# Moving attention masks in the DVE queue, and some copies, banks and biases of the first halves, in a fused attention and feed-forward kernel

## The chip, the cores and the metric

The kernel runs on one core of a Trainium2 chip. A core has a matrix engine (TensorE, PE in the profile), a vector engine (VectorE, DVE), a scalar engine (ScalarE, ACT), GpSimd (POOL) and a queue engine for transfers (SyncE, SP). Each works through its own instructions in the order in which they were written, and engines wait for one another by semaphores. Matrix products are written to banks of PSUM; all else lies in SBUF. The metric is the device time of one execution in microseconds; the median of ten runs is given.

## The reference

Attention over 4 batches of 8 heads with 768 positions of 64 numbers. A query sees the first 8 keys and the 96 keys that end at itself, with a slope on the distance; the heads' outputs, side by side, are rows of 512 for a gated feed-forward layer with 1536 inner columns.

```python
scores = scale * np.matmul(q, k.transpose(0, 1, 3, 2))
is_global = pos[None, :] < int(n_global)
is_local = (rel >= 0) & (rel < int(n_local))
keep = is_global | is_local
dist = np.where(is_global & ~is_local, float(n_local), np.abs(rel).astype(np.float32))
bias = -slopes[:, None, None] * dist[None, :, :]
scores = np.where(keep, scores + bias, -1000000000.0)
a = np.exp(scores - np.max(scores, axis=-1, keepdims=True))
a = a / (np.sum(a, axis=-1, keepdims=True) + 1e-09)
attn = np.matmul(a, v)
...
gate = np.maximum(x @ w_gate, 0.0)
val = x @ w_val
return (gate * val @ w_out).astype(np.float32)
```

## The kernel before

The work is cut into eight halves (`s` or `c`, 0 to 7): half a sequence of one batch, 384 queries. Within a half, heads go in four pairs (`p`), and the keys that a half's queries can see lie in tiles of 120 with the 8 global keys in front of each. The scores of one pair lie in three banks (`g`, 0 to 2) with keys on the partitions.

A pair passes these steps. Its q and k are cast to bf16 (`piece_cast`) and transposed: in half 0, 1 and 2 by PE (`piece_t`, L299) and copied out of PSUM (`piece_copy_k`, L278 to L284, `piece_copy_q`, L315), in halves 3 to 7 by transfers that transpose (`early_pieces`). Then come the scores. In half 0, and for pairs 0 and 3 of half 1, the bias is first put into the banks by products of a scaled identity with the distances (`piece_bias`, L327), scores are added on top (`piece_scores`, L342), and ScalarE takes the exponential (`piece_exp`, L359). Everywhere else `piece_qk` computes plain scores (L411) and the exponential (L414), and `piece_mask` (L429) multiplies by a table of exponentials of the bias on VectorE (`m_all`, made for each head by `setup_mask`, L245). Halves 0 and 1 do the product with the values and with ones by `piece_av_wide` (L480), take the sum's Ln and the exponential of its negative on ScalarE (`piece_ln_wide` L497, `piece_inverse_wide` L502), and VectorE multiplies (`piece_mul_wide`, L508) to give `xT`, the feed-forward input. From half 2 on `piece_av` (L445, L454, L459) and `piece_norm` (L465) do the same.

The feed-forward of a half is 12 steps `gate(fc)` and `val(fc)` of four products each (L531); ScalarE applies Relu (`grelu`, L540), VectorE multiplies into `ht` (L547), and then output products go over the 12 columns (L554, in the last block L569). `F0[2*fc]` and `F0[2*fc+1]` are gate and val of half 0; `gate[i]` and `val[i]` are the first four of them.

PSUM has eight banks in three pools: three for scores (`qk_psum`), two for values and transposes (`av_psum`), three for the feed-forward (`ff_psum`). A bank is used again when its last reader is done.

The order of every engine's work is the order of the calls. The first two halves are written out by hand call by call (from L627 on). After that `weave` puts items of attention between feed-forward steps by their share of the work: half 2's transposes (`T2`) with the feed-forward of halves 0 and 1; `attention_pieces(2)` with the end of these; then the attention of half c + 1 with the feed-forward of half c. In `attention_pieces` each item is one bank of scores with its mask, one value product, or one normalisation:

```python
return (QK(0) + QK(1) + AV(0) + N(0) + QK(2) + AV(1) + N(1) + g[0:1] + a[0:1] + g[1:2] + a[1:2]
        + N(2) + g[2:3] + [(0.0, lambda: None)] + AV(3) + N(3))
```

Loads come from two queues. SP loads q and k of half 0 and of halves 3 to 7. POOL issues, in this order: values of batch 0, part of q and k of half 1, the first quarter of the gate weights in two parts, the rest of q and k, the first part of the value weights (`wv0`), more values, the second and third parts of both weights, q and k of half 2, the output weights.

Of the kernel before, what the change touches and what calls it, by code (L numbers as in the profile page):

```python
# [8 lines left out]
FP32 = mybir.dt.float32  # L9
# [6 lines left out]
def kernel(  # L16
# [12 lines left out]
    nc = tc.nc  # L29
# [8 lines left out]
    HP = H // 2  # L38
# [13 lines left out]
    banks_of_half = [[], []]  # L52
# [191 lines left out]
    def setup_mask(h):  # L244
        nc.scalar.activation(m_all[:, h], dd, AF.Exp, bias=0.0, scale=-slopes[h])  # L245
# [42 lines left out]
    def piece_t(s, p, pool=av_psum, name="av_ps", apart=False):  # L288
        for i in (1, 0):
            if i == 1 or apart:  # L290
                tp = pool.tile([128, 512], FP32, name=name)
                tp = tp[:, 0:QH].bitcast(BF16).rearrange("d (i t) -> d i t", i=2)
            tp_of[s, p, i] = tp[:, i, :]
            for n in range(NN):
                for e in range(2 if s == 1 else 1):
                    r = slice(64 * e, 64 * e + 64) if s == 1 else slice(0, 128)
                    src = (qk16[s, i][:, 2 * p + e, n * D : (n + 1) * D] if s == 1
                           else cast_of[s, p][:, i, n])
                    nc.tensor.matmul(tp[r, i, n * 128 : (n + 1) * 128],  # L299
                                     lhsT=src, rhs=ident, is_transpose=True,  # L300
                                     start=((i == 1 or apart) and n == 0),
                                     stop=((i == 0 or apart) and n == NN - 1))

    def piece_copy_k(s, p):
        b, half = divmod(s, 2)
        put_keys(nc.vector.tensor_copy, nc.vector.tensor_copy, kT[b % 2][p], tp_of[s, p, 1], half)

    def piece_copy(s, p):
        piece_copy_k(s, p)
        piece_copy_q(s, p)  # L310

    def piece_copy_q(s, p, copy=nc.vector.tensor_copy):
        for e in range(2):
            r = slice(64 * e, 64 * e + 64)
            copy(qTb[s % 2][r, p, e, :], tp_of[s, p, 0][r, :])  # L315

    qk_of = {}

    def piece_bias(s, p):
        pool, name = (ff_psum, "ff_ps") if s == 0 and p % 2 else (qk_psum, "qk_ps")  # L320
        banks = [pool.tile([128, 512], FP32, name=name) for _ in range(3)]
        qk_of[s, p] = banks
        for g, bank in enumerate(banks_of_half[s % 2]):
            c = 0
            for i, (j, a, w, m) in enumerate(bank):
                for e in range(2):
                    nc.tensor.matmul(banks[g][:, c : c + NN * w], lhsT=sid[:, 2 * p + e],  # L327
                                     rhs=dd[:, 0 if j == 0 else 1, :, m : m + w],
                                     start=(i == 0 and e == 0), stop=False, skip_group_check=True)
                    c += NN * w  # L330
# [30 lines left out]
    def piece_biased(s, p):  # L361
        piece_scores(s, p)
        for g in range(3):
            piece_exp(s, p, g)
# [33 lines left out]
    def piece_qk(s, p, g, later=None):  # L398
        b, half = divmod(s, 2)
        kt = kT[b % 2][p]  # L400
        qd = qTb[s % 2][:, p].rearrange("d e (n p) -> d e n p", n=NN)
        bank = banks_of_half[half][g]
        cols = sum(2 * NN * w for _, _, w, _ in bank)
        ps = qk_psum.tile([128, 512], FP32, name="qk_ps")
        if g == 0:
            es01_of[s, p] = es_pool.tile([128, 2, 480], BF16, name="es01")
        es = es01_of[s, p][:, g] if g < 2 else es_pool.tile([128, 480], BF16, name="es2")
        c = 0
        for j, a, w, m in bank:
            n_ = 2 * NN * w  # L410
            nc.tensor.matmul(ps[:, c : c + n_], lhsT=kt[:, j, :],  # L411
                             rhs=qd[:, :, :, a : a + w], start=True, stop=True)
            c += n_
        nc.scalar.activation(es[:, 0:cols], ps[:, 0:cols], AF.Exp, bias=0.0, scale=scale)  # L414
        if later is None:
            piece_mask(s, p, bank, es)
        else:
            later.append(lambda: piece_mask(s, p, bank, es))
# [15 lines left out]
    def piece_av(s, p, e):  # L434
        b, half = divmod(s, 2)
        h = 2 * p + e
        vb = vbuf[b % 2]
        av = av_psum.tile([128, 512], FP32, name="av_ps")
        av_of[s, p, e] = av
        av3 = av[:, 0:QH].rearrange("d (n p) -> d n p", n=NN)  # L440
        todo = [t for bank in banks_of_half[half] for t in bank]
        for i, (j, a, w, m) in enumerate(todo):
            es, c = es_of[s, p, j, e]
            z0 = 2 * D * h + (D if e == 0 else 0)
            nc.tensor.matmul(av3[:, :, a : a + w],  # L445
                             lhsT=vb[:, j, z0 : z0 + 128],
                             rhs=es[:, c : c + NN * w].rearrange("k (n p) -> k n p", n=NN),
                             start=(i == 0), stop=(i == len(todo) - 1),
                             skip_group_check=True)
        o0, d0 = (0, 64) if e == 0 else (64, 0)  # L450
        if e == 0:
            av_of[s, p, "l"] = rc_pool.tile([128, QH], FP32, name="lnd")
        ln = av_of[s, p, "l"]
        nc.scalar.activation(ln[o0 : o0 + 64], av[d0 : d0 + 64, 0:QH], AF.Ln, bias=0.0, scale=1.0)  # L454
        if e == 1:
            if s not in xT_of:
                xT_of[s] = xt_pool.tile([128, N_DC, QH], BF16, name="xT")
            rc = rc_pool.tile([128, QH], FP32, name="rcp")
            nc.scalar.activation(rc, ln, AF.Exp, bias=0.0, scale=-1.0)  # L459
            av_of[s, p, "r"] = rc  # L460
            piece_norm(s, p, 0)
# [25 lines left out]
    def piece_norm_wide(s, p):  # L487
        piece_sums_wide(s, p)
        piece_mul_wide(s, p)
# [10 lines left out]
    def piece_inverse_wide(s, p):  # L500
        rc = rc_pool.tile([128, QH], FP32, name="rcp")
        nc.scalar.activation(rc, av_of[s, p, "l"], AF.Exp, bias=0.0, scale=-1.0)  # L502
        av_of[s, p, "r"] = rc

    def piece_mul_wide(s, p):
        if s not in xT_of:
            xT_of[s] = xt_pool.tile([128, N_DC, QH], BF16, name="xT")
        nc.vector.tensor_tensor(xT_of[s][:, p, :], av_of[s, p][1][:, 0:QH], av_of[s, p, "r"], op=ALU.mult)  # L508

    def attention_pieces(s):  # L510
        QK = lambda p: [(0.18, lambda g=g: piece_qk(s, p, g)) for g in range(3)]
        AV = lambda p: [(0.29, lambda e=e: piece_av(s, p, e)) for e in range(2)]
        N = lambda p: [(0.0, lambda: piece_norm(s, p, 1))]
        g = QK(3)
        a = AV(2)
        return (QK(0) + QK(1) + AV(0) + N(0) + QK(2) + AV(1) + N(1) + g[0:1] + a[0:1] + g[1:2] + a[1:2]
                + N(2) + g[2:3] + [(0.0, lambda: None)] + AV(3) + N(3))

# [94 lines left out]
    F0 = [f for _, f in f1_0]  # L615
# [5 lines left out]
    QKB, FFB, AVB = (qk_psum, "qk_ps"), (ff_psum, "ff_ps"), (av_psum, "av_ps")  # L621

    def AV(s, p, *pools):
        piece_av_wide(s, p, *pools)
        piece_norm_wide(s, p)
# [28 lines left out]
    piece_t(0, 2)  # L654
    cast(0, 3, A, A)
    piece_biased(0, 1)
    piece_bias(0, 2)
    piece_copy(0, 2)
    piece_t(0, 3)
    piece_biased(0, 2)  # L660
    piece_copy(0, 3)
    piece_bias(0, 3)
# [15 lines left out]
    def TC(s, p, *pool):  # L678
        piece_t(s, p, *pool)
        piece_copy(s, p)  # L680

    gate, val = F0[0:8:2], F0[1:8:2]
# [4 lines left out]
    piece_mul_wide(0, 0)  # L687
    piece_inverse_wide(0, 1)
    piece_inverse_wide(0, 2)
    piece_t(1, 0)  # L690
    piece_av_wide(0, 3, QKB, FFB)
    piece_ln_wide(0, 3)
    piece_copy_k(1, 0)
    piece_mul_wide(0, 1)
    piece_copy_q(1, 0)
    piece_inverse_wide(0, 3)
    piece_bias(1, 0)
    piece_t(1, 1)
    piece_mul_wide(0, 2)
    piece_mul_wide(0, 3)  # L700
    piece_copy(1, 1)
# [14 lines left out]
    masks = {p: [] for p in (1, 2)}  # L716
    for g in range(3):
        piece_qk(1, 1, g, masks[1])
    setup_mask(5)
    piece_copy(1, 2)  # L720
    gate[3]()
    piece_copy(1, 3)
    for g in range(3):
        piece_qk(1, 2, g, masks[2])
    for f in masks[1]:
        f()
    val[0]()
    piece_bias(1, 3)
    piece_biased(1, 3)
    val[1]()  # L730
    piece_av_wide(1, 0)
    piece_ln_wide(1, 0)
    piece_av_wide(1, 1, QKB)
# [13 lines left out]
    piece_inverse_wide(1, 2)  # L747
    piece_ln_wide(1, 3)
    piece_mul_wide(1, 2)
    piece_inverse_wide(1, 3)  # L750
    piece_mul_wide(1, 3)
    F0[9]()
    F0[10]()
    F0[11]()
    for p in range(HP):
# [7 lines left out]
    for p in range(HP):  # L763
        cast(2, p, P, P)
    load_v_half(2)
    T2 = [(0.0, lambda p=p: TC(2, p, *QKB)) for p in range(HP)]
    weave(f1_1[G[0]] + f1_0[G[1]][4:] + f1_1[G[1]],
          [(0.05 + 0.06 * j, lambda j=j: fill_ones(nc.vector, 0, j)) for j in range(NT)],
          [(0.1 + 0.2 * i, lambda h=h: setup_mask(h)) for i, h in enumerate((0, 1, 6, 7))],
# [50 lines left out]
```

## Time and profile before

| what | value |
|---|---|
| median of 10 runs | 247.32 us (247.06 to 248.03) |
| the profiled execution | 248.0 us, span 246.2 us |
| PE | 238.2 us busy, 97% of the span |
| ACT | 157.5 us, 64% |
| DVE | 135.5 us, 55% |
| POOL | 91.6 us, 37% |
| largest groups on PE | L531 gate 77.9 us, L531 val 77.9 us, L554 63.2 us |
| chain that ended last | PE 85%, DVE 4%, DMA 4%, POOL 3%, ACT 2% |

The span runs from the first to the last instruction; the execution's own time is 1.8 us longer. The sum of busy times of one engine counts products that overlap in the pipeline only once, but the mean duration of a product (326 ns for 128x384) holds its way through the array as well; the distance between two starts is what it costs. The granted clock of PE is full in every part of the span. An idle time in brackets in a timeline names the engine and tile that ended it.

### The profile page before, as it was taken

The numbers are of one execution on the slowest core, as the hardware profiler recorded it, in microseconds if no ns is written. First come the engines' busy times: TensorE is split into PE (matmuls) and PEld (weight loads), VectorE is DVE, ScalarE is ACT, GpSimd is POOL, SyncE is SP. The second block draws the span as 40 slices with busy tenths as digits, with TensorE's granted clock in tenths as the row PEclk, the third lists the DMA queues.
The fourth block names the chain that finished last, engine by engine and source line by source line (L and its number), as shares of the span: only waits on it lengthen the run. The fifth ranks groups of instructions, "written<-read, shape, count | busy, mean of one in ns | idle before, by whom it ended". The sixth has DMA issues, their size and how long they took to land.

```text
span 246.2 us, 4850 instructions
## 1 busy us (share of the span) xinstructions
PE 238.2 (97%) x1739; PEld 143.5 (58%) x1739; DVE 135.5 (55%) x355; ACT 157.5 (64%) x329; POOL 91.6 (37%) x213
## 2 busy tenths in 40 slices
PE   7888999999999999999999999999999999999994
PEld 3674666656454666556654666556665666556644
DVE  6877757966531566336762567427663466523410
ACT  7998764377553877567774877567774778553311
POOL 8996944924680076302546063503620000000000
PEclk9999999999999999999999999999999999999999
DMA  6999999997699776838359959838431100020012
GB/s 179 194 166 183 207 289 232 146 103 244 146 168 173 232 120 151 92 91 252 82 114 98 265 153 147 77 104 258 108 85 70 60 0 3 4 110 18 0 43 86
DMA packets 76536, 32.35 MB, mean 131 GB/s; under 512 B 55424, under 2 KB 73216, under 8 KB 76512
## 3 DMA queue, kind: packets, MB, share of 16 engines
q0 software_dynamic: 34896, 10.27, 37.4%
q1 hardware_dynamic: 41616, 21.78, 33.4%
q8 instruction: 13, 0.21, 0.4%
q14 instruction: 11, 0.09, 0.1%
HBM read 28.38 MB, written 6.29 MB: 141 GB/s over the span
## 4 chain that ended last, share of the span: by engine, by line
PE 85%; DVE 4%; DMA 4%; POOL 3%; ACT 2%; issue 1%; POOLq 0%; DVEq 0%
PE ff_ps L531 47%; PE ff_ps L554 24%; PE av_ps L445 6%; PE qk_ps L411 5%; DMA wg<-in_moe_w_gate_dram 4%; DVE ht L547 2%; POOL vbuf L149 1%; ACT es L414 1%; PE ff_ps L569 1%; DVE qT L315 1%; PE av_ps L480 1%; DVE kT L278 1%; PE qk_ps L480 1%; PE av_ps L299 0%; POOL ks L126 0%
## 5 line engine op out<-in xcount | busy, mean ns | idle before, releaser
L531 PE MATMUL ff_ps<-xT,wg 128*128 128x384 bf16 x384 | 77.9, 326 | 0.8 <-DMA wg<-in_moe_w_gate_dram 0.4
L531 PE MATMUL ff_ps<-xT,wv 128*128 128x384 bf16 x384 | 77.9, 326 | 0.0
L540 ACT ACTIVATE grelu<-ff_ps 128x384 bf16<-128x384 f32 x96 | 46.7, 488 | 34.5 <-PE ff_ps L531 16.8
L547 DVE TENSOR_TENSOR ht<-ff_ps,grelu 128x384 bf16<-128x384 f32 x96 | 53.1, 554 | 23.6 <-PE ff_ps L531 22.0
L554 PE MATMUL ff_ps<-wo_sb,ht 128*128 128x512 bf16 x276 | 63.2, 379 | 0.5 <-DVE ht L547 0.5
L429 DVE TENSOR_TENSOR es<-es,m_all 128x432 bf16<-128x432 bf16 (+5 forms) x118 | 33.7, 316 | 34.6 <-ACT es L414 33.2
L531 PEld LDWEIGHTS <-wg 128*128 128x128 bf16 x384 | 35.9, 97 | 23.5 <-issue 1.0
L531 PEld LDWEIGHTS <-wv 128*128 128x128 bf16 x384 | 36.4, 98 | 22.3 <-DMA wv<-in_moe_w_val_dram 0.2
L414 ACT ACTIVATE es<-qk_ps 128x432 bf16<-128x432 f32 (+2 forms) x78 | 41.0, 532 | 8.2 <-PE qk_ps L411 6.0
L465 DVE TENSOR_TENSOR xT<-av_ps,rcp 64x384 bf16<-64x384 f32 x48 | 26.7, 555 | 33.8 <-ACT rcp L459 21.1
L554 PEld LDWEIGHTS <-ht 128*128 128x128 bf16 x276 | 26.0, 97 | 28.6 <-issue 0.6
L454 ACT ACTIVATE lnd<-av_ps 64x384 f32<-64x384 f32 x48 | 23.3, 485 | 13.3 <-PE av_ps L445 12.5
L367 POOL CAST kc<-ks 128x384 bf16<-128x384 f32 x20 | 9.5, 520 | 57.7 <-DMA ks<-in_k_dram 57.7
L559 ACT COPY osb<-ff_ps 128x512 f32<-128x512 f32 x23 | 13.5, 585 | 24.5 <-PE ff_ps L554 24.3
L411 PE MATMUL qk_ps<-qT,kT 128*128 128x432 bf16 (+5 forms) x118 | 26.7, 286 | 0.1
L149 POOL DMA_DIRECT2D vbuf<-in_v_dram x29 | 24.8, 872 | 0.0
L445 PEld LDWEIGHTS <-vbuf 128*128 128x128 bf16 x216 | 17.8, 98 | 6.4
L445 PE MATMUL av_ps<-es,vbuf 128*128 128x216 bf16 (+4 forms) x216 | 20.5, 226 | 0.0
L411 PEld LDWEIGHTS <-kT 128*128 128x128 bf16 x118 | 11.4, 98 | 8.1
L375 POOL CAST qz<-qs 128x192 bf16<-128x192 f32 x40 | 12.8, 369 | 3.7 <-DMA qs<-in_q_dram 3.7
L459 ACT ACTIVATE rcp<-lnd 128x384 f32<-128x384 f32 x24 | 12.5, 522 | 0.8
L278 POOL COPY kT<-kN 128x360 bf16<-128x360 bf16 x8 | 4.4, 547 | 7.7 <-DMA kN<-kc 7.7
(107 smaller groups left out, 154.0 us busy)
## 6 DMA issues: line engine op xcount, KB each, us to landing
out_dram<-osb SPq DMA_DIRECT2D x23, 256.0 KB
ks<-in_k_dram SPq DMA_DIRECT2D x5, 768.0 KB
qs<-in_q_dram SPq DMA_DIRECT2D x5, 768.0 KB
vbuf<-in_v_dram POOLq DMA_DIRECT2D x23, 120.0 KB, 4.9
wv<-in_moe_w_val_dram POOLq DMA_DIRECT2D x3, 512.0 KB, 10.9
wo_sb<-in_moe_w_out_dram POOLq DMA_DIRECT2D x1, 1536.0 KB, 21.5
wg<-in_moe_w_gate_dram POOLq DMA_DIRECT2D x2, 512.0 KB, 10.6
ks<-in_k_dram SPq DMA_DIRECT2D x4, 192.0 KB
```

Source lines behind the costliest of these rows:

```text
L149: nc.gpsimd.dma_start(out=v_dst(b, NG + r0, NG + r0 + n, j), in_=v[b, :, KT * j + r0 : KT * j + r0 + n, :].rearrange("h p d -> p h d"))
L411: nc.tensor.matmul(ps[:, c : c + n_], lhsT=kt[:, j, :], rhs=qd[:, :, :, a : a + w], start=True, stop=True)
L414: nc.scalar.activation(es[:, 0:cols], ps[:, 0:cols], AF.Exp, bias=0.0, scale=scale)
L429: nc.vector.tensor_mul(e4, e4, mk)
L445: nc.tensor.matmul(av3[:, :, a : a + w], lhsT=vb[:, j, z0 : z0 + 128], rhs=es[:, c : c + NN * w].rearrange("k (n p) -> k n p", n=NN), star ...
L454: nc.scalar.activation(ln[o0 : o0 + 64], av[d0 : d0 + 64, 0:QH], AF.Ln, bias=0.0, scale=1.0)
L465: nc.vector.tensor_tensor(xT_of[s][r, p, :], av_of[s, p, e][r, 0:QH], av_of[s, p, "r"][r], op=ALU.mult)
L531: nc.tensor.matmul(st[key][:, 0:QH], lhsT=w_of(w, dc, fc), rhs=xT_of[c][:, dc, :], start=(dc == 0), stop=(dc == N_DC - 1))
L540: nc.scalar.activation(gr, psg[:, 0:QH], AF.Relu, bias=0.0, scale=1.0)
L547: nc.vector.tensor_tensor(ht[:, fc, :], psv[:, 0:QH], st["r", fc], op=ALU.mult)
L554: nc.tensor.matmul(ps2, lhsT=ht[:, fc, n * 128 : (n + 1) * 128], rhs=wo_sb[:, fc, :], start=(fc == 0), stop=(fc == N_FC - 1))
L559: nc.scalar.copy(osb, ps2)
```

## The change

Four things are changed.

- In `attention_pieces` the mask products of a bank are no longer written right after its exponential, but kept in a list, and written after the scores and the exponential of the next bank, or ahead of the next value product (`flush`). The empty item ahead of the last pair's value products becomes a `flush`. This concerns halves 2 to 7.
- The transposes of half 2 use two banks for a pair, one for k and one for q (`apart=True`), and q is copied out by ScalarE instead of VectorE.
- In half 1, pair 0's transposes go to a bank of `qk_psum` instead of `av_psum`; its q copy comes ahead of half 0's xT product of pair 1; pair 1's transposes come ahead of pair 0's bias. In half 0 the third bank of pair 2's bias is written after pair 3's transposes.
- `val[1]` comes ahead of the bias and scores of half 1's pair 3, the mask table of head 5 after the exponentials of pair 2, and `F0[9]` (`val(4)` of half 0) ahead of the last inverse and xT product of half 1; on PE its place stays the same, on DVE its ht product now stands ahead of that xT product.

The instructions of PE are as many as before. ACT has eight copies more and DVE eight fewer. The orders of POOL and SP are the same.

```diff
-    def piece_bias(s, p):
+    def piece_bias(s, p, groups=(0, 1, 2)):
...
-        for g, bank in enumerate(banks_of_half[s % 2]):
+        for g in groups:
+            bank = banks_of_half[s % 2][g]
...
     def attention_pieces(s):
-        QK = lambda p: [(0.18, lambda g=g: piece_qk(s, p, g)) for g in range(3)]
-        AV = lambda p: [(0.29, lambda e=e: piece_av(s, p, e)) for e in range(2)]
+        masks = []
+
+        def qk(p, g):
+            ready = masks[:]
+            masks.clear()
+            piece_qk(s, p, g, masks)
+            for f in ready:
+                f()
+
+        def flush():
+            for f in masks:
+                f()
+            masks.clear()
+
+        QK = lambda p: [(0.18, lambda g=g: qk(p, g)) for g in range(3)]
+        AV = lambda p: [(0.29, lambda e=e: (flush(), piece_av(s, p, e))) for e in range(2)]
...
-                + N(2) + g[2:3] + [(0.0, lambda: None)] + AV(3) + N(3))
+                + N(2) + g[2:3] + [(0.0, flush)] + AV(3) + N(3))
...
-    piece_bias(0, 2)
+    piece_bias(0, 2, (0, 1))
     piece_copy(0, 2)
     piece_t(0, 3)
+    piece_bias(0, 2, (2,))
...
-    piece_t(1, 0)
+    piece_t(1, 0, *QKB)
     piece_av_wide(0, 3, QKB, FFB)
     piece_ln_wide(0, 3)
-    piece_copy_k(1, 0)
+    piece_copy(1, 0)
     piece_mul_wide(0, 1)
-    piece_copy_q(1, 0)
     piece_inverse_wide(0, 3)
+    piece_t(1, 1)
     piece_bias(1, 0)
-    piece_t(1, 1)
...
-    setup_mask(5)
     piece_copy(1, 2)
     gate[3]()
     piece_copy(1, 3)
     for g in range(3):
         piece_qk(1, 2, g, masks[2])
+    setup_mask(5)
     for f in masks[1]:
         f()
     val[0]()
+    val[1]()
     piece_bias(1, 3)
     piece_biased(1, 3)
-    val[1]()
...
     piece_mul_wide(1, 2)
+    F0[9]()
     piece_inverse_wide(1, 3)
     piece_mul_wide(1, 3)
-    F0[9]()
...
-    T2 = [(0.0, lambda p=p: TC(2, p, *QKB)) for p in range(HP)]
+
+    def T2_piece(p):
+        piece_t(2, p, *QKB, apart=True)
+        piece_copy_k(2, p)
+        piece_copy_q(2, p, nc.scalar.copy)
+
+    T2 = [(0.0, lambda p=p: T2_piece(p)) for p in range(HP)]
```

More of the change, by code (lines that the diff above doesn't have):

```diff
@@ L317 @@
     qk_of = {}
-    def piece_bias(s, p):
+    def piece_bias(s, p, groups=(0, 1, 2)):
         pool, name = (ff_psum, "ff_ps") if s == 0 and p % 2 else (qk_psum, "qk_ps")
-        banks = [pool.tile([128, 512], FP32, name=name) for _ in range(3)]
-        qk_of[s, p] = banks
-        for g, bank in enumerate(banks_of_half[s % 2]):
+        if (s, p) not in qk_of:
+            qk_of[s, p] = [pool.tile([128, 512], FP32, name=name) for _ in range(3)]
+        banks = qk_of[s, p]
+        for g in groups:
+            bank = banks_of_half[s % 2][g]
             c = 0
```

## The prediction

> **What bounds the kernel now.** I read the page's busy table first, then the windows, then the timelines of TensorE (PE), VectorE (DVE) and ScalarE (ACT) around every place where PE pauses. One line of the page and three windows:
>
> ```profile
> PE 238.2 (97%) x1739; PEld 143.5 (58%) x1739; DVE 135.5 (55%) x355; ACT 157.5 (64%) x329; POOL 91.6 (37%) x213
> ```
>
> ```profile
> 41.95:50.44 8.49, 8.27 (x66) 5.34 (x65) 8.05 (x28) 3.12 (x8) 8.49 (x13) 1.00 1.48 153
> 50.44:62.06 11.62, 11.16 (x75) 6.94 (x75) 7.31 (x19) 8.89 (x19) 3.55 (x10) 1.00 1.00 180
> ...
> 108.10:240.30 132.20, 132.20 (x865) 78.22 (x864) 68.87 (x164) 83.43 (x170) 29.41 (x80) 1.00 0.43 98
> ```
>
> The columns of a window are its length, then busy time and count of PE, weight loads, DVE, ACT and POOL, the granted clock, DMA share and GB/s. PE sets the time. Since a busy PE need not be at its peak, I go by the distance from one start to the next: four 128x384 products take 0.65 us wherever nothing is waited for (163 ns each), and that holds from 62.06 us to 240.3, where PE waits for nobody. So no reordering can win anything there; it can only win in the first 62 us. There I add up what PE loses, beginning here:
>
> ```profile
> 23.58 0.81 PE L531 MATMUL ff_ps<-xT,wv 128*128 128x384 bf16 x4
> 24.69 1.23 PE L327 MATMUL qk_ps<-dd,sid 128*128 128x72 bf16 x10 [0.30 <-ACT es L414]
> 25.76 0.75 PE L342 MATMUL qk_ps<-qT,kT 128*128 128x144 bf16 x5
> 26.35 0.81 PE L531 MATMUL ff_ps<-xT,wv 128*128 128x384 bf16 x4
> 27.09 0.50 PE L480 MATMUL av_ps<-es,ones 128*64 128x72 bf16 x10
> ...
> 33.20 0.81 PE L531 MATMUL ff_ps<-xT,wv 128*128 128x384 bf16 x4
> 34.15 0.81 PE L531 MATMUL ff_ps<-xT,wg 128*128 128x384 bf16 x4
> ...
> 49.87 0.35 PE L411 MATMUL qk_ps<-qT,kT 128*128 128x432 bf16 x1
> 50.44 0.81 PE L531 MATMUL ff_ps<-xT,wg 128*128 128x384 bf16 x4 [0.22 <-DVE ht L547]
> ```
>
> The reader is to see starts that come later than the one before plus its length. The last bias (24.69) waits for exponentials that free its banks and takes 1.07 us instead of about 0.65; 34.15 comes 0.30 after 33.20 + 0.65; 50.44 comes 0.39 after 49.87 + 0.18. A further 0.10 is lost at 48.58. The last loss is at 62.06, where the first output product should follow at 61.45: 0.61 us, for a bank that DVE frees:
>
> ```profile
> 60.28 0.56 DVE L465 TENSOR_TENSOR xT<-av_ps,rcp 64x384 bf16<-64x384 f32 x1
> 60.87 0.55 DVE L429 TENSOR_TENSOR es<-es,m_all 128x432 bf16<-128x432 bf16 x1
> 61.45 0.56 DVE L547 TENSOR_TENSOR ht<-ff_ps,grelu 128x384 bf16<-128x384 f32 x1
> ```
>
> A mask (L429) stands ahead of the ht product (L547) that frees the bank.
>
> **Last bias and val[1].** Products are only swapped, so PE's own work is unchanged. val[0] starts at 23.58 as before, since its weights land then (issued 12.55, landing 10.9 later). val[1] follows to 24.88. Meanwhile ACT does the exponentials of pair 2 without the mask table of head 5 ahead of them; in the trace that table (23.22) takes 0.45 of queue, and the three exponentials ended at 25.5, so they end at about 25.05, and the last bank is needed near 25.3: no wait. Ten bias products cost 0.65 (eight took 0.55 at 7.10), the scores 0.59, so the next block starts at 24.88 + 0.65 + 0.59 + the 0.09 that it had = 26.2 instead of 27.09: gain 0.89. It needs values that land at 26.0 (issued 18.8, 7.2 to landing) only 0.4 after its start. The moved table is ready near 25.5; its reader, the masks of pair 2 on DVE, comes after 26.
>
> **F0[9] ahead of the last normalisation.** F0[9] started at 31.89; with the gain it would start at 31.0, but its weights land at 31.1 (issued 20.50, 10.6) and a product started 0.13 after such a landing at 23.58: 31.23, gain left 0.66. The three products end at 33.18. Before, the next one waited 0.30 for F0[9]'s ht, which stood behind the last xT product (33.07 to 33.63). Now ht runs in the time in which xT waits for its reciprocal, and xT is needed only by the fourth product. So 0.30 is won: gain 0.96, next start 33.19.
>
> **The third half's transposes.** The first stood at 41.95, now at 40.99. What is late next is a load: q of this half lands at 40.77 and POOL's cast of its first pair runs from 40.78 to 41.29. Three k transposes run to 41.16, the q ones start at 41.35, and the block ends at 41.52 instead of 42.28: gain 0.76. The load's issue was itself held 0.42 by an exponential that now ends earlier; that could give up to 0.4 back, which I leave out of the sum. Then eight q copies leave DVE, 0.35 each, 2.8 of the 8.05 us it was busy in the 8.49 us window; DVE had 1.9 us of work in each 1.63 us round, now 1.2. The 0.10 and 0.39 go: gain 0.49. On ACT each copy costs 0.464 (the two of the first half). A round there is a relu and a pair of copies, 0.45 + 0.95 = 1.4 of 1.63, and once a mask table of 0.5, 0.3 over; that relu comes late, but its bank is asked for only a product later, over 0.3 away. Between 0 and 0.3 I take 0, as the cover is larger. Two banks for each transpose instead of one: the second's q needs the first's k copied, 0.6 us of DVE work in 1.3 us.
>
> **Queued masks, half 2.** In DVE's new order the ht at 61.45 stands right behind the xT at 60.28, hence 60.87 to 61.43, and PE goes on at 61.48 instead of 62.06 less shift: 0.57 of the 0.61.
>
> **Queued masks, halves 3 to 7.** A gain is excluded by the window to 240.3. A loss would be a value product that finds its mask late. The closest is the last pair's third mask: now one slot (about 1 us) ahead of its reader instead of two. But in both orders it stands right after the same two xT products on DVE, so it starts no later. Ends: 0 and one whole mask (0.5) for each of six halves, 3.0; I take 0.
>
> **First and second half, before 19.5 us.** The transposes of pair 0 need no longer wait 0.63 for a Ln, the bias of pair 0 waits instead for the q copy (16.4), the split bias lets three transposes wait up to 0.2 for ACT's cast. All of it lies ahead of the gate weights, which land at 19.46 (issued 10.36, 9.1). PE reaches them about 18.4 by these rows, so 1.0 us of cover; without it each would count in full. POOL's and SP's orders, and so all loads, are unchanged.
>
> **The sum.** 0.76 + 0.49 + 0.57 = 1.82 us. Against the profiled execution: 248.0 - 1.8 = 246.2, its span 246.2 - 1.8 = 244.4, 1.8 lying around it. That execution is 0.7 above the median of ten, so the median becomes 247.32 - 1.82 = 245.5.
>
> **A rule weighed.** The rows above say that late loads take 10 to 15 us: q of the third half, issued 25.77, lands 15.0 later, and this swallows 0.20 of the gain. The Trainium skill, "DMA: Bandwidth & Descriptors", section Anatomy of one DMA, fits a transfer by 2.0 us plus bytes over 436 GB/s: for 768 KB an estimate of 3.8 us. By it neither load would hold anything, F0[9] would start at 31.0 and the sum would be 0.89 + 0.30 + 0.49 + 0.57 = 2.25 us, 245.1. The fit is for one transfer; here many share the engines, so the rows decide.
>
> **Rivals.** *Loads decide* (0.13): everything up to 42 us is held by the transfers, which share one another's time, and arriving earlier wins nothing. For it: PE sits on landings at 19.46 and 23.45 already. Against: the q row allows 0.76. Then 0.49 + 0.57: 246.3. *ScalarE becomes the gate* (0.08): the copies delay relus, the 0.49 is not won and 0.3 comes on top: 247.32 - 0.76 - 0.57 + 0.3 = 246.3. Against it: 3.12 busy of 8.49. *Waits are replaced* (0.08): at each place another operand is late, under 0.5 won: 247.0. For it: several margins are 0.1 to 0.4 us. *Late masks, slower* (0.09): in halves 2 to 7 the value products of the last pair wait for the third mask. It outweighs 1.82 from 0.30 a half on; at 0.4 it is 6 x 0.4 - 1.82 = +0.6: 247.9. For it: ACT is 63% busy there and the mask waits for its exponential; against it: the same DVE neighbours.
>
> **How the numbers follow.** The forecast has 0.62, with its own range 244.9 (no load holds) to 246.1. What this kernel's measurement can tell from no change is about 0.2%, 0.5 us. Faster: 0.62 + 0.13 + 0.08 = 0.83; same 0.08; slower 0.09. The range takes in the first three cases with 0.3 for unknown ends: 244.8 to 246.6; about 0.17 lies outside.
>
> **What would show it.** Right: the normaliser products of the second half start near 26.2; the first product of its second stage near 33.2; no wait between the third half's transposes and its scores; the output product follows without a DVE wait; after 62 us everything is the same, shifted. Wrong: PE waits after 62 us for L429's masks, or a transpose at 41 us that waits longer than 0.2 for POOL.

## The result and the profile after

The changed kernel takes 246.0 us (median of 16 runs, 245.47 to 246.45). The kernel before, run beside it, takes 247.38 us (58 runs). The ratio is 0.9939, with a 95% interval from 0.9931 to 0.9948. The gain is 1.38 us by medians, where 1.82 was forecast. The profiled execution took 245.88 us, span 244.1, so it stands for the median well; the profiled execution of before, 248.0, did not.

The page's busy line and the windows that answer to those of before (length, then busy time and count of PE, weight loads, DVE, ACT, POOL, the granted clock, DMA share, GB/s), and under them the window of before that answers to the third:

```profile
PE 237.1 (97%) x1739; PEld 143.1 (59%) x1739; DVE 132.7 (54%) x347; ACT 161.0 (66%) x337; POOL 91.2 (37%) x213
```

```profile
39.81:48.56 8.75, 8.24 (x66) 5.37 (x65) 5.88 (x19) 6.62 (x15) 8.47 (x14) 1.00 1.42 176
48.56:59.57 11.01, 11.01 (x77) 6.87 (x76) 6.86 (x18) 8.68 (x18) 3.17 (x6) 1.00 1.24 192
59.57:77.61 18.04, 17.87 (x103) 9.01 (x101) 6.32 (x15) 9.17 (x18) 10.11 (x26) 1.00 1.01 167
106.00:238.15 132.15, 132.15 (x864) 78.15 (x863) 68.11 (x164) 83.42 (x170) 29.17 (x80) 1.00 0.43 98
```

```profile
62.06:79.75 17.69, 17.68 (x100) 8.98 (x100) 5.80 (x14) 8.75 (x18) 8.64 (x21) 1.00 1.03 163
```

Eight q copies have gone from DVE (8.05 us busy before, now 5.88, in the first window) to ACT (3.12, now 6.62). The second window is as long as PE needs: 11.01 of 11.01. The third is new to the story: it was 17.69 long before and is 18.04 now.

The timeline of PE, where the reader should again look for starts that come later than the start before plus its products:

```profile
22.54 1.46 PE L547 MATMUL ff_ps<-xT,wv 128*128 128x384 bf16 x8
23.83 0.77 PE L329 MATMUL qk_ps<-dd,sid 128*128 128x72 bf16 x10
24.45 0.76 PE L344 MATMUL qk_ps<-qT,kT 128*128 128x144 bf16 x5
25.13 0.50 PE L482 MATMUL av_ps<-es,ones 128*64 128x72 bf16 x10
...
31.36 0.81 PE L547 MATMUL ff_ps<-xT,wv 128*128 128x384 bf16 x4
32.01 0.81 PE L547 MATMUL ff_ps<-xT,wg 128*128 128x384 bf16 x4
...
39.81 0.33 PE L299 MATMUL qk_ps<-ident,qk 128*128 128x128 bf16 x3
40.65 0.34 PE L299 MATMUL qk_ps<-ident,qk 128*128 128x128 bf16 x3 [0.51 <-POOL qk L263]
...
48.38 0.35 PE L413 MATMUL qk_ps<-qT,kT 128*128 128x432 bf16 x1
48.56 0.81 PE L547 MATMUL ff_ps<-xT,wg 128*128 128x384 bf16 x4
```

The last bias no longer waits (ten products in 0.62). The step from 31.36 to 32.01 is 0.65, PE's own pace, where 0.95 stood before. The q transposes at 40.65 wait for POOL's cast of a late load: by the starts 40.65 - 39.97 = 0.68. The wait behind the first scores is gone. On DVE the `ht` product now stands ahead of the mask, and the first output product (59.57) follows the last scores without a wait:

```profile
58.36 0.56 DVE L467 TENSOR_TENSOR xT<-av_ps,rcp 64x384 bf16<-64x384 f32 x1
58.95 0.56 DVE L563 TENSOR_TENSOR ht<-ff_ps,grelu 128x384 bf16<-128x384 f32 x1
59.42 0.40 DVE L431 TENSOR_TENSOR es<-es,m_all 128x432 bf16<-128x432 bf16 x1
```

Then comes a loss that was not there before. The chain of waits shows it (start, length, what):

```profile
65.94 0.40 ACT osb L575
66.34 3.00 DMA out_dram<-osb
...
69.42 0.58 ACT osb L575
70.00 0.36 ACT es L416
70.36 0.02 issue
70.39 0.32 DVE es L431
70.71 0.04 issue
70.75 0.27 PE av_ps L447 x2
```

ACT copies each finished output tile into `osb`, and SP stores it. There are two `osb` tiles, so the third copy must wait until the first store has landed, at 69.34 (66.34 + 3.00). The chain names the second copy (65.94) ahead of the store, but the store is that of the first tile: in the kernel before it went out at 66.90, ahead of the second copy at 68.44. Behind that copy on ACT stands the exponential of half 2's last bank, behind it the mask on DVE, behind that the value product: by starts PE loses 0.35 us here (18.04 - 17.69). The first and the third copy on ACT, before and then after:

```profile
65.40 0.58 ACT L559 COPY osb<-ff_ps 128x512 f32<-128x512 f32 x1
...
71.49 0.58 ACT L559 COPY osb<-ff_ps 128x512 f32<-128x512 f32 x1 [0.97 <-PE ff_ps L554]
```

```profile
62.90 0.58 ACT L575 COPY osb<-ff_ps 128x512 f32<-128x512 f32 x1
...
69.42 0.58 ACT L575 COPY osb<-ff_ps 128x512 f32<-128x512 f32 x1 [1.39 <-DMA out_dram<-osb]
```

Why was the store late? Here is SP's queue before, and then after:

```profile
53.40 0.38 SPq L111 DMA_DIRECT2D ks<-in_k_dram  x1
...
60.18 3.91 SPq L378 DMA_TRANSPOSE kN<-kc  x3
64.20 2.59 SPq L382 DMA_TRANSPOSE qT<-qz  x2
66.90 0.52 SPq L560 DMA_DIRECT2D out_dram<-osb  x1
67.47 2.44 SPq L382 DMA_TRANSPOSE qT<-qz  x1
```

```profile
52.68 0.38 SPq L111 DMA_DIRECT2D ks<-in_k_dram  x1
...
59.62 3.91 SPq L380 DMA_TRANSPOSE kN<-kc  x3
63.64 2.60 SPq L384 DMA_TRANSPOSE qT<-qz  x2
66.34 0.93 SPq L576 DMA_DIRECT2D out_dram<-osb  x1
67.32 1.28 SPq L384 DMA_TRANSPOSE qT<-qz  x1
```

The store stands on SP behind five transposes of half 3, which wait for that half's k and q to be loaded and cast. SP can issue those loads only behind copies of values (from 47.66), whose values POOL loads (from 43.24, landed at 47.59) behind its casts of half 2's q, which landed at 40.03. So this queue keeps the time of the loads: its store moved 0.56 us earlier (66.90 to 66.34), while the first `osb` copy, which keeps PE's time, moved 2.50 (65.40 to 62.90). Before, the third copy began at 71.49 and waited only for PE. If the store took 3.0 us there too, it landed at about 69.9 and 1.6 us were to spare (an estimate); 2.50 - 0.56 = 1.94 is more than that by 0.35.

### The profile page after: what moved, and what is told of

Read it like the earlier page. It is cut to its first block, busy times and chain, and to the rows that moved or that the text cites. A ratio compares the mean times of both kernels' runs of the same rounds, so it can differ in the third digit from the quotient of the medians.

```text
span 244.1 us, 4883 instructions
## 1 busy us (share of the span) xinstructions
PE 237.1 (97%) x1739; PEld 143.1 (59%) x1739; DVE 132.7 (54%) x347; ACT 161.0 (66%) x337; POOL 91.2 (37%) x213
## 4 chain that ended last, share of the span: by engine, by line
PE 82%; DMA 9%; ACT 4%; DVE 2%; SPq 1%; issue 1%; POOL 0%; DVEq 0%; ACTq 0%
PE ff_ps L547 46%; PE ff_ps L570 23%; DMA qs<-in_q_dram 8%; PE av_ps L447 5%; PE qk_ps L413 5%; DMA out_dram<-osb 1%; ACT es L361 1%; PE ff_ps L585 1%; SPq L111 1%; ACT lnd L499 1%; DVE es L431 1%; PE qk_ps L299 1%; ACT qk L263 1%; DVE qT L315 1%; ACT kN L361 0%
## 5 line engine op out<-in xcount | busy, mean ns | idle before, releaser
L431 DVE TENSOR_TENSOR es<-es,m_all 128x432 bf16<-128x432 bf16 (+5 forms) x118 | 32.1, 315 | 3.9 <-ACT es L416 3.6
L377 POOL CAST qz<-qs 128x192 bf16<-128x192 f32 x40 | 12.3, 356 | 2.5 <-DMA qs<-in_q_dram 2.5
L282 POOL COPY kT<-kN 128x240 bf16<-128x240 bf16 x12 | 5.0, 416 | 7.3 <-DMA kN<-kc 4.6
```

The lines of the kernel that those rows point to most:

```text
L431: nc.vector.tensor_mul(e4, e4, mk)
```

## The experiments

All times are medians of 5 to 16 runs; the kernel before ran beside each. To compare traces I cut them at products that every kernel has. "Scores to output" is from the first scores of half 2 to the first output product, "output block" from there to the first gate product of the next block, "rest" from there to the last product but a few. The third `osb` copy would come 6.09 after the first if it waited for PE alone.

| kernel | us | ratio, 95% interval | scores to output | output block | rest | third `osb` copy after the first |
|---|---|---|---|---|---|---|
| before (first run) | 247.32 | 1 | 12.19 | 17.69 | 160.54 | 6.09 |
| changed | 246.0 | 0.9939, 0.9931 to 0.9948 | 11.19 | 18.04 | 160.54 | 6.52 |
| masks only | 246.91 | 0.9987, 0.9974 to 1.0001 | 11.58 | 17.68 | 160.54 | 6.09 |
| transposes only | 247.25 | 0.9994, 0.9982 to 1.0006 | 11.64 | 17.69 | 160.54 | 6.09 |
| the same again | 247.22 | 0.9994, 0.9976 to 1.0012 | 11.89 | 17.91 | 160.54 | 6.39 |
| hand-written part only | 246.52 | 0.9968, 0.9956 to 0.9979 | 11.98 | 17.69 | 160.54 | 6.11 |
| masks and transposes | 246.75 | 0.9969, 0.9957 to 0.9981 | 11.19 | 18.37 | 160.54 | 6.84 |
| masks queued in half 2 only | 245.94 | 0.9951, 0.9933 to 0.9969 | 11.19 | 18.00 | 160.81 | 6.47 |
| first half's edits undone | 246.28 | 0.9952, 0.9937 to 0.9966 | 11.19 | 18.64 | 160.54 | 7.11 |
| third half's q loaded earlier | 246.8 | 0.9972, 0.9958 to 0.9985 | 11.19 | 18.75 | 160.54 | 7.23 |
| three output tiles | 245.49 | 0.9922, 0.9910 to 0.9934 | 11.19 | 17.69 | 160.53 | 6.09 |
| three tiles, q earlier | 245.9 | 0.9938, 0.9915 to 0.9960 | 11.19 | 17.69 | 160.54 | 6.09 |
| transposes one item later | 247.17 | 0.9988, 0.9968 to 1.0007 | 11.18 | 19.54 | 160.54 | 8.00 |
| three tiles, transposes later | 245.1 | 0.9907, 0.9885 to 0.9930 | 11.36 | 17.68 | 160.54 | 6.09 |

### Each part alone

The kernel before, with the queued masks of `attention_pieces` alone:

```diff
-        QK = lambda p: [(0.18, lambda g=g: piece_qk(s, p, g)) for g in range(3)]
-        AV = lambda p: [(0.29, lambda e=e: piece_av(s, p, e)) for e in range(2)]
+        QK = lambda p: [(0.18, lambda g=g: qk(p, g)) for g in range(3)]
+        AV = lambda p: [(0.29, lambda e=e: (flush(), piece_av(s, p, e))) for e in range(2)]
...
-                + N(2) + g[2:3] + [(0.0, lambda: None)] + AV(3) + N(3))
+                + N(2) + g[2:3] + [(0.0, flush)] + AV(3) + N(3))
```

> The kernel before with the new queueing of masks in halves 2 to 7 and nothing else. Theory: only the stall ahead of the first output product goes (0.61 us, 0.57 of it won), and no value product waits for a mask, since PE is too little ahead for the store of an output tile to be late: 247.4 - 0.6 = 246.8, profile without a wait of L554 for ht and without a wait of an av product for es. Rival, late masks by themselves: a value product near 72 us waits about 0.3 for its mask here too, gain 0.2 to 0.3: 247.1.

With the third half's transposes in two banks and its q copied by ScalarE alone:

```diff
-    T2 = [(0.0, lambda p=p: TC(2, p, *QKB)) for p in range(HP)]
+    def T2_piece(p):
+        piece_t(2, p, *QKB, apart=True)
+        piece_copy_k(2, p)
+        piece_copy_q(2, p, nc.scalar.copy)
+
+    T2 = [(0.0, lambda p=p: T2_piece(p)) for p in range(HP)]
```

> The kernel before with only half 2's transposes in two banks and q copied by ScalarE. Theory: the 0.10 and 0.39 us between 48 and 50.5 us go, the stall at 62 stays: 246.9. Rival, ScalarE becomes the gate: PE waits for a relu or a copy between 42 and 50 us, gain under 0.2: 247.2 or more.

With the edits written by hand in the first two halves alone:

```diff
     val[0]()
+    val[1]()
     piece_bias(1, 3)
     piece_biased(1, 3)
-    val[1]()
...
     piece_mul_wide(1, 2)
+    F0[9]()
     piece_inverse_wide(1, 3)
     piece_mul_wide(1, 3)
-    F0[9]()
```

(and the moves of half 0's and half 1's first transposes and biases as in the change)

> The changed kernel with masks and half 2's transposes as before: only the edits in halves 0 and 1 remain. Theory: PE reaches half 2's first transposes 0.9 to 1.0 us earlier and waits there for the load of q, the DVE lag and the stall at 62 stay: gain 0.5 to 0.8, 246.6 to 246.9. Rival, loads decide everything: gain under 0.2. The three single gains together should exceed the 1.4 of all at once by about 0.35 if the wait for the late output store comes only when all are joined.

Measured against 247.33: masks 0.42 won, transposes 0.08, hand-written part 0.81; together 1.31, against 1.38 for the whole. By the clock only the hand-written part is clear of no change (0.5 to 1.1 by its interval); the intervals of the other two hold the ratio 1, and what they win is read from their traces. The masks alone take the whole 0.61 from the first output product (12.19 to 11.58), and the other two lengths stay as they were. In the trace of the hand-written part PE still meets what the other two parts remove, and the load at the transposes:

```profile
40.87 0.34 PE L299 MATMUL qk_ps<-ident,qk 128*128 128x128 bf16 x3 [0.70 <-POOL qk L263]
49.07 0.81 PE L533 MATMUL ff_ps<-xT,wg 128*128 128x384 bf16 x4 [0.17 <-DVE ht L549]
60.53 1.46 PE L556 MATMUL ff_ps<-wo_sb,ht 128*128 128x512 bf16 x6 [0.30 <-DVE ht L549]
```

The transposes were the miss: the trace showed 0.55 us won from scores to output, but the clock only 0.08. So this kernel was run again.

> The same kernel as the one with the transposes' edit alone, measured again. By the starts of the products (0.10 and 0.39 of waits gone, 0.14 less at the output product) it must be 0.55 below the kernel before: 246.8 us. The first measurement gave 0.1 to 0.15. If that was scatter of the first loads, this one comes nearer to 246.8; if it is again above 247.1, the 0.55 is given back somewhere that the one profiled execution does not show.

247.22 against 247.45, interval from 0.9976 to 1.0012: again next to nothing. Neither half of the expectation fits. The profile of this second execution shows a place where the gain goes in that execution: scores to output 11.89 (0.30 won instead of 0.55), and the output block 17.91 (0.22 lost to the store). From the transposes to the next block the first execution won 0.59, the second 0.12. With the old order of the masks, `ht` waits behind a mask that took 0.38 in one execution and 0.63 in the other; the last section returns to it. That all executions lose the gain in this way is not shown by two profiles.

### Masks and transposes without the hand-written part

The two diffs above together.

> Kernel before with the queued masks and the third half's transposes as in the change, and none of the edits written by hand in the first two halves. Theory (the terms add, and the wait for a store appears only when the first halves run earlier): 0.49 + 0.61 gone, nothing lost near 70 us, 246.3 us. Rival (each alone measured 0.1 to 0.45, and they add as measured): 246.9 us. If the store wait appears here too, it belongs to the masks or the copies and not to the earlier start.

246.75, with 0.70 won, between theory and rival. Up to the first output product the terms do add: 12.19 to 11.19. But the store wait is there as well (18.37, 0.68 lost). That was not expected: an earlier start by the hand-written edits is not needed for it, only that PE reaches the output products sooner than the loads allow the store (60.41 us instead of 62.06, with the store at 66.78 as against 66.90).

### Is it the queued masks of the later halves?

```diff
             masks.clear()
+            if s > 2:
+                return piece_qk(s, p, g)
             piece_qk(s, p, g, masks)
```

> The changed kernel with masks queued in half 2 only, halves 3 to 7 as before. Theory: no PE wait lies there, so the same as the changed kernel within 0.15: 246.0, and the 0.33 wait of half 2's last pair stays. Rival, queueing costs or saves something in each half: 5 halves x 0.1 or more, 245.5 or 246.5.

245.94, the same as the changed kernel. With the old order in halves 3 to 7 the rest is 160.81 instead of 160.54, one gap of 0.28, ahead of a gate product at 80.86 that waits for an `ht` product; the kernel before, with the old order in every half, has no such gap. In halves 3 to 7 the late masks that the slower rival feared cost nothing in any kernel with the new order.

### Is it the store?

```diff
-    osb_pool = ctx.enter_context(tc.tile_pool(name="osb", bufs=2))
+    osb_pool = ctx.enter_context(tc.tile_pool(name="osb", bufs=3))
```

> The changed kernel with three output tiles in SBUF instead of two. Theory: ScalarE's third output copy no longer waits 1.4 us for a store, the exponential behind it comes 0.43 earlier, and the value product near 70.7 us no longer waits 0.33 for its mask: 246.0 - 0.33 = 245.7. Rival, the mask is late by its own place in the queue: the wait stays, 246.0.

245.49 us, 0.5 below the changed kernel, and the output block is back at 17.69. The masks stand where they stood. ACT's third copy now waits for PE, and then PE's value products follow one another:

```profile
69.03 0.59 ACT L575 COPY osb<-ff_ps 128x512 f32<-128x512 f32 x1 [0.97 <-PE ff_ps L570]
```

```profile
68.98 1.46 PE L570 MATMUL ff_ps<-wo_sb,ht 128*128 128x512 bf16 x6
70.27 0.42 PE L447 MATMUL av_ps<-es,vbuf 128*128 128x216 bf16 x4
```

So the loss in the output block is that of the two output tiles, shown by taking it away. (By the clock alone the 0.5 is not clear of the scatter: the two ratios' intervals just overlap, 0.9934 and 0.9931.)

### Is the load of the third half's q worth moving?

Its load was put ahead of the third part of the weights on POOL, first with two output tiles and then with three:

```diff
     load_w_group(1)
-    load_w_group(2)
     load_qk(2, 0, H, nc.gpsimd)
+    load_w_group(2)
```

> The changed kernel with q and k of half 2 loaded ahead of the third parts of the weights (which are needed only from 47 us on). Theory: the q transposes near 40.6 us no longer wait 0.5 for POOL's cast; what follows is 0.5 earlier, if the store near 66 us does not take it back: 245.5 to 245.9. Rival, the load was not the limit there: 246.0.

> The changed kernel with both: three output tiles and the early load of q and k. Theory: 246.0 - 0.33 - 0.5 = 245.2. If the gains share one cause: 245.6.

246.8 and 245.9 us. The first cast of q now runs at 35.48 instead of 40.09, and the transposes wait for nothing. But others arrive later, and with two tiles the store wait grows, as PE's timeline shows:

```profile
28.36 0.82 PE L547 MATMUL ff_ps<-xT,wg 128*128 128x384 bf16 x4 [0.43 <-DMA wg<-in_moe_w_gate_dram]
30.94 0.82 PE L547 MATMUL ff_ps<-xT,wv 128*128 128x384 bf16 x4 [0.39 <-DMA wv<-in_moe_w_val_dram]
71.67 0.27 PE L447 MATMUL av_ps<-es,vbuf 128*128 128x144 bf16 x2 [0.88 <-DVE es L431]
```

Weights wait 1.16 by starts (0.60 and 0.56) where 0.68 was to be won, and the store takes 1.06. With three tiles the second loss is gone; 245.9 is not to be told from 245.49 by the intervals.

### Do the edits ahead of the gate weights matter?

```diff
-    piece_bias(0, 2, (0, 1))
+    piece_bias(0, 2)
...
-    piece_bias(0, 2, (2,))
...
-    piece_t(1, 0, *QKB)
+    piece_t(1, 0)
...
-    piece_copy(1, 0)
+    piece_copy_k(1, 0)
     piece_mul_wide(0, 1)
+    piece_copy_q(1, 0)
     piece_inverse_wide(0, 3)
-    piece_t(1, 1)
     piece_bias(1, 0)
+    piece_t(1, 1)
```

> The changed kernel with the first two edits undone: pair 0's transposes of half 1 in the value pool again, its q copy and the bias in the old order, the split bias of half 0 whole. Theory: all of it lies ahead of the landing of the gate weights, PE arrives there 0.6 later, and the landing at 18.3 to 19.5 and the load of q at 40 us swallow it: 246.0, at most 246.2. Rival, the cover is thin when loads land early: up to 246.5.

246.28. The third half's transposes end at 40.76 as against 40.83, so nothing was given up before them: these edits are worth nothing there, as forecast. But the cover is not where the prediction had it. PE comes to the gate weights 0.49 later than in the changed kernel (17.79 instead of 17.30) and does not wait for them; `val[0]` starts 0.19 later (22.73 instead of 22.54), and only the wait for q at the transposes takes that up (0.37 instead of 0.51). In the output block of the profiled execution the store wait was 0.95 (18.64), which is more than the 0.28 that the median lies higher. That the edits cause it is not shown: this wait differs between executions of the same kernel too, as the two runs of the transposes alone tell.

### Transposes one item later

The transposes wait for q at 40.65, so their items were spread from 0.59 to 0.99 of the block instead of 0.55 to 0.95; one more feed-forward step then runs ahead of each. With two tiles and with three:

```diff
-          spread(T2, 0.55, 0.95))
+          spread(T2, 0.59, 0.99))
```

> Changed kernel with the third half's transposes one item later, two output tiles as in the change. Theory (whatever arrives earlier at the output tiles waits there for the store): the wait for POOL's cast at 40.65 us goes, and the wait for the store grows by as much; 245.9 to 246.0 us, the same as the changed kernel. Rival (the store's wait does not grow): 245.6 us.

> Changed kernel with three output tiles instead of two, and the third half's transposes spread over 0.59 to 0.99 of the block instead of 0.55 to 0.95, so that each pair stands one item later. Theory (the load of the third half's q still holds its transposes by 0.35 to 0.6 us, and the store wait is removed by the third tile): no wait for POOL's cast at the transposes, no wait for a mask near 69 us, 0.4 below the three-tile kernel: 245.1 us. Rival (what the transposes no longer lose is lost later, because their copies now end closer to the scores that read them): the block from the transposes to the scores grows by the same 0.4, and the time stays at 245.5.

With three tiles 245.1 us, as the theory said; its interval overlaps that of three tiles alone, but it is the lowest time of all. The wait for q is gone, 0.17 of it comes back between scores and output. With two tiles the edit is a loss of 1.2: 247.17. Both theory and rival were wrong here, as both took the store to land as before. In the profile the chain reads:

```profile
57.83 2.02 POOL kc L369 x4
...
63.89 1.24 SPq L384
...
65.17 2.74 SPq L384
...
68.02 2.38 DMA out_dram<-osb
...
70.47 0.59 ACT osb L575
71.06 0.36 ACT es L416
...
71.44 0.32 DVE es L431
...
71.80 0.27 PE av_ps L447 x2
```

The first output product came 0.44 earlier (59.13), and the store was issued 1.7 later: one transposing transfer held SP 2.74 us where its neighbour held it 1.24. That makes 1.85 lost in the output block (19.54). Such a long transpose is no mark of this kernel: in each of the fourteen traces two or three of the 30 transposing transfers held SP for 1.65 to 2.76 us, where most took 1.20 to 1.31. In the kernel before one of them, at 67.47, stands just behind the first store, where it does no harm. In four profiled executions it stands just ahead of that store, which is then issued 3.7 to 4.1 after the first q transpose instead of 2.7 (this kernel, three tiles with later transposes, three tiles with earlier q, first half's edits undone). With three tiles it costs nothing. What makes a transpose long, and what puts it ahead of the store, stays open; no wait in the traces names it. So how much of the 1.2 belongs to the later transposes themselves is open too.

## Why the prediction was right, and where its terms were off

The time of 246.0 lay in the range and the direction was right, 0.5 above the forecast. Yet both of the prediction's own signs of being wrong came: a transpose at 41 us waited 0.68 for POOL, where 0.2 was the limit, and PE waited once after 62 us for a mask. The two cost so little that the time stayed in the range. By steps:

- **Last bias and val[1].** From `val[0]` to the normaliser products 3.51 became 2.59; the working gave 2.62. Right.
- **F0[9].** The wait of 0.30 behind it is gone (0.65 from start to start). It waits for its own weights, as forecast (0.23 in the trace, landed at 30.00). Right.
- **The third half's transposes.** The mechanism was right: q's load holds them, and from its cast to the end of the block it took 0.74, in the working and in the trace. The size rested on one execution's landings, and the wait was too small: 0.19 was allowed, 0.68 came. `val[0]` started 1.04 us earlier than in the profiled execution of before (its weights landed at 22.28 instead of 23.43), q's cast only 0.69 earlier. In the five profiled executions with the first halves of before, the block ended 0.34 to 2.20 us after the earliest end that q's cast allowed (0.76 in the one that the prediction read); in the changed kernel and in the four others that move `val[1]` and `F0[9]` but not q's load or the transposes (hand-written part only, masks queued in half 2 only, first half's edits undone, three output tiles), 0.00. What the term is worth on average is known only roughly. The hand-written part alone wins 0.81 by medians, of which its trace shows 0.30 behind the transposes (0.09 up to the scores and 0.21 from scores to output); that leaves about 0.5, and 0.2 to 0.8 by the interval, so the forecast 0.76 is not excluded. The possible 0.4 from an earlier issue of that load, left out of the sum, did not come: the issue was still held 0.36.
- **DVE's lag and queued masks, half 2.** 0.49 and 0.57 were forecast, together 1.06. From the end of the transposes to the first output product 19.78 became 18.74: 1.04. Right. ScalarE did not become the gate: up to the scores 7.59 became 7.55.
- **Halves 3 to 7.** 160.54 before and after. Right at zero.
- **The first halves, before 19.5 us.** Right at zero, by the kernel that undoes them, but for another reason: what covers them is q's load, not the gate weights. The second part of these landed at 19.45 in the execution that the prediction read, and at 17.28 to 17.84 in the four others with the first halves of before, where PE did not wait for it. The cover of 1.0 there was one execution's chance. In detail one thing differed too: the last six products of pair 0's bias, at 16.31, wait for a Ln and not for the q copy.
- **What failed.** In the step on the halves' masks the last value products were priced at 0, because the mask stands behind the same two xT products on DVE. The mask indeed starts late in half 2, at the place that the slower rival named, but by another way: store, `osb` copy, exponential, mask. It is paid once and not per half: 0.35 in the profile, 0.5 by the median of three tiles against two. The prediction noted that POOL's and SP's orders are unchanged and took that for no cost. It did not ask which of SP's transfers would be too late for a PE that comes 2 us sooner.

With the two corrections the sum is 0.5 + 1.04 - 0.35 = 1.2 us, against 1.38 measured; with 0.76 in place of the 0.5 it is 1.45. Without the store wait the kernel with three tiles wins 1.97 (interval 1.6 to 2.2), which holds the 1.82 of the forecast. Of the rivals, that loads decide was in part true, twice over: at q's transposes, and through half 3's load at the store.

The rule that was weighed, the Trainium skill, "DMA: Bandwidth & Descriptors", section Anatomy of one DMA, would have let q land 3.8 us after its issue, an estimate by its fit for a single transfer. In the trace after, it took 15.4 us (24.58 to 40.03), with loads of weights under way beside it (landed at 27.46 to 47.41). The measurement decides; for a load queued among others the fit was no guide here.

## What to carry to other kernels

An unchanged queue is no safe queue. When the engine that sets the time gets faster, list the transfers that do not move with it, and compare for each the old distance between its landing and its reader with the planned gain: here 1.6 us were to spare and 1.94 were used. A third buffer at the output is a cheap way to take such a link out. With it the later transposes read 0.4 lower by medians, which the intervals do not separate from nothing; without it they lost 1.2, in the profiled execution together with a transfer that held SP longer for a reason that stays open.

## What the runs showed of the hardware

The same mask product on DVE (L431, or L429; 128x432, bf16) does not always take the same time. In the changed kernel from 40 us on, all 27 that ran while POOL computed nothing took 0.37 to 0.38 us; of the nine that ran beside a POOL cast or copy three took as little, and six took 0.40 to 0.72. In the kernel before it is 0.37 to 0.39 alone, and up to 0.55 beside POOL. In all fourteen traces a mask over 0.40 lay beside POOL's work. The Trainium skill, "SBUF — State Buffer", section Who interferes with whom, says that VectorE and GpSimd share one pair of ports, taken as an exclusive lock; that the long ones all lie beside POOL agrees with it, and that some masks beside POOL are not longer shows that overlap alone does not decide. The two executions of the transposes alone are of both kinds: the mask that `ht` waits behind took 0.63 beside POOL's casts of k, and 0.38 beside its casts of q. It was seen in these traces and not tried by itself.

The landing of the first loads differs by one to two microseconds between executions in which they were issued at the same time: the second part of the gate weights, issued at 10.34 to 10.36, landed at 19.45, 17.43, 17.28, 17.34 and 17.84 us in the five executions whose first halves are those of before, and `val[0]` started at 23.58, 24.09, 23.03, 22.75 and 22.97. So a difference between two profiled executions up to 42 us says little below 1 us; the distances behind it, and medians, say more.
